# A decode kernel's extra w2 row: four transfers into a rotated buffer in place of three into its own, and one VectorE operation fewer per attention output

## The chip, the cores and the metric

One core of one Trainium2 chip runs the kernel. The metric is the device time of that core in microseconds, the median of several executions. The kernel before takes 135.47 us (three executions: 135.47 to 135.51). The profile of one more execution, of 135.52 us, shows a span of 133.7 us from the first to the last instruction; all positions below are microseconds from the start of that span.

## The reference

A single decode step for two batch rows of width 576: layer norm of `x`, then attention over a cached window and a dense MLP with a squared ReLU, both from the same normed input, and everything is added up.

```python
W = min(4096, max(256, Sk // 4))                 # 2048 of Sk = 8192 cached positions
q = (xn @ wq).reshape(B, 1, 32, 128)             # B = 2, 32 query heads on 16 kv heads
k, v = k_cache[:, :, Sk-W:], v_cache[:, :, Sk-W:]  # each (2, 16, 2048, 128) bf16
p = softmax(q . k * 128 ** -0.5)
a = (p . v).reshape(B, 1, 4096) @ wo             # wo 4096 x 576
h = relu(xn @ w1 + b1); h = h * h                # w1 576 x 4608
m = h @ w2 + b2                                  # w2 4608 x 576
out = x + a + m
```

All inputs and the output are bf16. Keys and values come to 33.6 MB, the four weight matrices to 20 MB, and each byte is read once.

## The kernel before

Attention is cut into eight units `u` of four kv heads and one batch row. Each unit has one key tile and one value tile of 2 MB, in a pool of six. The large transfers are issued on the queue of SyncE (SP), the small ones on ScalarE's (ACT).

```python
XS = [(0, 85), (85, 117), (117, 128)]
W2P = [(0, 9), (9, 14), (14, 16), (16, 17)]       # pieces of the second half of w2
...
kvpool = ctx.enter_context(tc.tile_pool(name="kvpool", bufs=6))
keep = ctx.enter_context(tc.tile_pool(name="keep", bufs=2))
...
const.tile([P, 112], F32, name="pad_0")
w2x_sb = const.tile([P, D], BF16, name="w2x_sb")  # D = 576: 1152 bytes in each of 128 rows
xb_sb = const.tile([B + 1, D], BF16, name="xb_sb")
nc.scalar.dma_start(out=x_sb, in_=x2d)            # two rows
load_k(0); wq_sb = issue_flat(A_wq, "wq"); load_k(1); load_v(0); load_k(2); load_v(1); load_k(3)
...
def softmax(u):
    ...                                           # row maxima, exponentials into p_sb
    pT = keep.tile([P, NJJ, SR], BF16, tag="pT", name=f"pT_{u}")
    nc.vector.transpose(out=pT[:].rearrange("p j r -> p (j r)"), in_=p_sb[:])
...
def fin():                                        # the end of one unit: normalise, spread into ws
    op = psum.tile([P, Dh + 1], F32, tag="op", name=f"op_ps_{u}")
    matmul(op[pp, :], lhsT=of_h[:], rhs=o1[:], ...)
    nc.vector.reciprocal(out=linv[pp, :], in_=op[pp, Dh:Dh + 1])
    mk = work.tile([P, WC], F32, tag="mk", name=f"mk_{u}")
    nc.vector.tensor_scalar(out=mk[pp, :], in0=own_c[pp, :], scalar1=linv[pp, 0:1], ...)
    nc.vector.tensor_tensor(out=om, in0=op[pp, 0:Dh]..., in1=mk[pp, :]...to_broadcast([32, WC, WR]), op=ALU.mult)
    nc.vector.tensor_reduce(out=ws[pp, :, BS * b], in_=om..., op=ALU.add)
```

The main sequence. `step(u)` transposes the keys of unit `u` on TensorE, multiplies the probabilities of unit `u - 2` by its values, and computes scores and softmax of `u`.

```python
softmax(0)
load_v(2)
for i in range(0, 2 * NG4, 4):                    # b1: 8 rows of 1152 bytes, four at a time
    nc.scalar.dma_start(out=b1_sb[i:i + 4, :], in_=b1_rows[i:i + 4, :])
nc.scalar.dma_start(out=xb_sb[B:B + 1, :], ...)   # b2: one row
for p0, p1 in XS:                                 # the extra row of w2
    nc.scalar.dma_start(out=w2x_sb[p0:p1, :], in_=w2_rows[1, p0:p1, (FR - 1) * D:FR * D])
step(1)
...
for u in range(2, NU - 1):
    step(u)
    ...                                           # v, k and, at u == 4, w1 issued as buffers come free
mlp_h(w1_sb)
wo_sb = issue_flat(A_wo, "wo")
...                                               # w2a, w2b and three pieces of w2c issued
step(NU - 1)
pv_all(NU - 2)
out_acc(hT_sb[:, 1, FR - 1, :], w2x_sb, 0)        # the one use of w2x_sb
pv_all(NU - 1)
for r in range(WR):
    out_acc(ws[:, r, :], wo_sb, r)
for r in range(FR):
    out_acc(hT_sb[:, 0, r, :], w2a_sb, r)
for r in range(FR - 1):
    w, o = (w2b_sb, r) if r < r9 else (w2c_sb, r - r9)
    out_acc(hT_sb[:, 1, r, :], w, o, stop=(r == FR - 2))
nc.scalar.copy(out=fin_sb[:], in_=out_ps[:])
nc.scalar.dma_start(out=..., in_=fin_sb[0:RM:BS, :])
```

Of the kernel before, what the change touches and what calls it, by code (L numbers as in the profile page):

```python
# [8 lines left out]
F32 = mybir.dt.float32  # L9
BF16 = mybir.dt.bfloat16  # L10
ACT = mybir.ActivationFunctionType
ALU = mybir.AluOpType
# [4 lines left out]
def kernel(  # L17
# [14 lines left out]
    nc = tc.nc  # L32
    P = 128
    B, Sq, D = A_x.shape
    _, Hkv, Sk, Dh = A_k_cache.shape
# [19 lines left out]
    NJJ = NJ // NS  # L55
    SR = NS * NC
# [4 lines left out]
    NG4 = 4  # L61
# [10 lines left out]
    WR = Hq * Dh // P  # L72
    WC = Dh // WR
    FR = L1 // P
    assert HW == 32 * FR and QH * 2 == NC and NC * WC == 32
    W2P = [(0, 9), (9, 14), (14, 16), (16, 17)]
    XS = [(0, 85), (85, 117), (117, 128)]
    BS = 16
    MB = BS * (B - 1) + 1
    RM = 32 * (NG4 - 1) + MB  # L80
# [3 lines left out]
    const = ctx.enter_context(tc.tile_pool(name="const", bufs=1))  # L84
# [4 lines left out]
    work = ctx.enter_context(tc.tile_pool(name="work", bufs=2))  # L89
    keep = ctx.enter_context(tc.tile_pool(name="keep", bufs=2))  # L90
# [22 lines left out]
    def load_v(u):  # L113
        issue_kv(v_tiles, A_v_cache, u, "v")

    def issue_flat(w, name):
# [2 lines left out]
        nc.sync.dma_start(out=tl[:, 0:n], in_=w.rearrange("r n -> (r n)").rearrange("(p l) -> p l", p=P))  # L119
        return tl  # L120

    const.tile([P, 112], F32, name="pad_0")
    w2x_sb = const.tile([P, D], BF16, name="w2x_sb")
    xb_sb = const.tile([B + 1, D], BF16, name="xb_sb")
    x_sb = xb_sb[0:B, :]
    nc.scalar.dma_start(out=x_sb, in_=x2d)
# [16 lines left out]
                                 op0=ALU.mult, op1=ALU.add)  # L143
# [3 lines left out]
    for q in range(4):  # L147
        nc.vector.tensor_scalar_add(out=row_f[32 * q:32 * (q + 1), :], in0=row32[32 * q:32 * (q + 1), 0:1],
                                    scalar1=float(32 * q))
# [21 lines left out]
    for k in range(NK):  # L171
        nc.vector.tensor_scalar(out=xn_sb[:, k, :].rearrange("b (m c) -> b m c", c=2), in0=x_v[:, :, k:k + NK:NK - 1],  # L172
                                scalar1=mv[:, 0:1], scalar2=rstd[:, 0:1], op0=ALU.subtract, op1=ALU.mult)
# [7 lines left out]
    for t0, half, k0, n, pc in ((0, 0, 0, NK, 0), (0, 1, 0, NK, 1), (1, 0, 1, NK - 1, 1), (1, 1, 0, NK - 1, 0)):  # L181
        nc.vector.tensor_scalar(out=xnT[:, t0:NH:2, half, :], in0=pro_ps[:, k0:k0 + n, :], scalar1=par[:, pc:pc + 1],
                                scalar2=None, op0=ALU.mult)
# [3 lines left out]
    own_c = const.tile([P, WC], F32, name="own_c")  # L187
# [5 lines left out]
                          in_=own[:].unsqueeze(2).to_broadcast([P, NC, WC]))  # L193
    in_s = const.tile([P, NS], F32, name="in_s")
    nc.vector.tensor_reduce(out=in_s[:], in_=ident[:].rearrange("p (g s c) -> p s g c", s=NS, c=NC), axis=AX.XY,
                            op=ALU.add)
    far_h = const.tile([TH, P], BF16, name="far_h")
    nc.vector.tensor_scalar(out=far_h[:].rearrange("p (a h r) -> p a h r", h=TH, r=rep),
                            in0=ident[0:TH, 0:TH].unsqueeze(1).unsqueeze(3).to_broadcast([TH, P // NC, TH, rep]),
# [87 lines left out]
    def softmax(u):  # L287
        sc_ps = sc_tiles.pop(u)
        m1 = work.tile([P, 1], F32, tag="m1", name=f"m1_{u}")
        nc.vector.tensor_reduce(out=m1[:], in_=sc_ps[:], axis=AX.X, op=ALU.max)  # L290
        m2 = work.tile([P, NC], F32, tag="m2", name=f"m2_{u}")
        nc.vector.tensor_scalar(out=m2[:], in0=off[:], scalar1=m1[:, 0:1], scalar2=None, op0=ALU.add)  # L292
        gmax = work.tile([P, NC], F32, tag="gmax", name=f"gmax_{u}")
        nc.gpsimd.partition_all_reduce(gmax[:], m2[:], channels=P, reduce_op=ReduceOp.max)  # L294
        gown = work.tile([P, NC], F32, tag="gown", name=f"gown_{u}")
        bias = work.tile([P, 1], F32, tag="bias", name=f"bias_{u}")
        nc.vector.scalar_tensor_tensor(out=gown[:], in0=gmax[:], scalar=-scale, in1=own[:], op0=ALU.mult,  # L297
                                       op1=ALU.mult, accum_out=bias[:])
        p_sb = work.tile([P, NJJ * 32], BF16, tag="p_sb", bufs=1, name=f"p_{u}")
        o1 = keep.tile([P, Dh + 1], F32, tag="o1", name=f"o1_{u}")  # L300
        nc.scalar.activation(out=p_sb[:], in_=sc_ps[:], func=ACT.Exp, bias=bias[:, 0:1], scale=scale,  # L301
                             accum_out=o1[:, Dh:Dh + 1])
        pT = keep.tile([P, NJJ, SR], BF16, tag="pT", name=f"pT_{u}")
        nc.vector.transpose(out=pT[:].rearrange("p j r -> p (j r)"), in_=p_sb[:])  # L304
        pT_tiles[u] = pT
        o1_tiles[u] = o1
# [18 lines left out]
    def pv_end(u):  # L325
        tq, b = divmod(u, B)
        o_ps = o_tiles.pop(u)
        o1 = o1_tiles.pop(u)
        for k in range(NS):
            kw = dict(out=o1[:, 0:Dh], in0=o_ps[:, k * Dh:(k + 1) * Dh])  # L330
            if k == 0:
                nc.vector.tensor_scalar(scalar1=in_s[:, 0:1], scalar2=None, op0=ALU.mult, **kw)  # L332
            else:
                nc.vector.scalar_tensor_tensor(scalar=in_s[:, k:k + 1], in1=o1[:, 0:Dh], op0=ALU.mult, op1=ALU.add,  # L334
                                               **kw)

        def fin():
            op = psum.tile([P, Dh + 1], F32, tag="op", name=f"op_ps_{u}")
            pp = slice(32 * tq, 32 * (tq + 1))
            matmul(op[pp, :], lhsT=of_h[:], rhs=o1[:], start=True, stop=True, skip_group_check=True,  # L340
                   tile_position=(0, 32 * tq))
            linv = work.tile([P, 1], F32, tag="linv", name=f"linv_{u}")
            nc.vector.reciprocal(out=linv[pp, :], in_=op[pp, Dh:Dh + 1])
            mk = work.tile([P, WC], F32, tag="mk", name=f"mk_{u}")
            nc.vector.tensor_scalar(out=mk[pp, :], in0=own_c[pp, :], scalar1=linv[pp, 0:1], scalar2=None, op0=ALU.mult)
            om_t = work.tile([P, Dh], F32, tag="om", name=f"om_{u}")
            om = om_t[pp, :].rearrange("p (q r) -> p q r", r=WR)
            nc.vector.tensor_tensor(out=om, in0=op[pp, 0:Dh].rearrange("p (q r) -> p q r", r=WR),
                                    in1=mk[pp, :].unsqueeze(2).to_broadcast([32, WC, WR]), op=ALU.mult)
            with nc.allow_low_precision(reason="sums of one term and zeros"):  # L350
                nc.vector.tensor_reduce(out=ws[pp, :, BS * b], in_=om.rearrange("p q r -> p r q"), axis=AX.X,
                                        op=ALU.add)

        return fin

    def mlp_h(w1_sb):
        h_ps = [psum.tile([P, HB], F32, tag="kT", bufs=3, name=f"h_ps_{k}") for k in range(2)]
        for k in range(2):
            matmul(h_ps[k][:], lhsT=sel_h[:], rhs=b1_sb[:, k * HB:(k + 1) * HB], start=True, stop=False,
                   skip_group_check=True)  # L360
        for t in range(NH):
            for k in range(2):
                for g in range(NG4):
                    o = t * L1 + g * HW + k * HB
                    matmul(h_ps[k][32 * g:32 * g + 2 * B, :],
                           lhsT=xnT[:, t].rearrange("p x b -> p (x b)"), rhs=w1_sb[:, o:o + HB], start=False,
                           stop=(t == NH - 1), skip_group_check=True, tile_position=(0, 32 * g))
        hrow = const.tile([RB, 4 * HW], BF16, tag="row", name="hrow")
        h4 = hrow[:].rearrange("p (a n) -> p a n", a=4)
        for k in range(2):  # L370
            t1_t = work.tile([P, HB], F32, tag="t1", name=f"t1_{k}")
            t1 = t1_t[0:RB, :]
            nc.scalar.activation(out=t1, in_=h_ps[k][0:RB, :], func=ACT.Relu)  # L373
            t4 = t1.unsqueeze(1).to_broadcast([RB, 4, HB])
            nc.vector.tensor_tensor(out=h4[:, :, k * HB:(k + 1) * HB], in0=t4, in1=t4, op=ALU.mult)  # L375
        nr = FR // 2
        for a in range(2):
            hp = psum.tile([P, nr, RB + 4], BF16, tag="sc", bufs=2, name=f"hp_{a}")
            for r in range(nr):
                transpose(out=hp[:, r, 0:RB], in_=hrow[:, a * nr + r:4 * HW:FR], identity=ident[0:RB, 0:RB])  # L380
            for g in range(NG4):
                pp = slice(32 * g, 32 * (g + 1))
                cp = nc.scalar.copy if g % 2 else nc.vector.tensor_copy
                cp(out=hT_sb[pp, :, a * nr:(a + 1) * nr, 0:MB:BS].rearrange("p x r b -> p r x b"),
                   in_=hp[pp, :, 32 * g:32 * g + 2 * B].rearrange("p r (x b) -> p r x b", b=B))
# [28 lines left out]
    softmax(0)  # L414
    load_v(2)
    b1_rows = B_b1.rearrange("(x n) -> x n", n=HW)
    for i in range(0, 2 * NG4, 4):
        nc.scalar.dma_start(out=b1_sb[i:i + 4, :], in_=b1_rows[i:i + 4, :])
    nc.scalar.dma_start(out=xb_sb[B:B + 1, :], in_=B_b2.rearrange("(o n) -> o n", o=1))
    for p0, p1 in XS:  # L420
        nc.scalar.dma_start(out=w2x_sb[p0:p1, :], in_=w2_rows[1, p0:p1, (FR - 1) * D:FR * D])
    step(1)
    load_k(4)
    out_acc(sel_b[:], xb_sb, 0, start=True)
    for u in range(2, NU - 1):
        step(u)
        if u + 1 < NU - 2:
            load_v(u + 1)
        if u == 4:
            w1_sb = issue_flat(B_w1, "w1")  # L430
        if u + 3 < NU:
            load_k(u + 3)
        if u == 5:
            for v in (NU - 2, NU - 1):
                load_v(v)
    mlp_h(w1_sb)
    wo_sb = issue_flat(A_wo, "wo")
    w2a_sb = w2pool.tile([P, FR * D], BF16, name="w2a")
# [52 lines left out]
```

## Time and profile before

| what | before |
|---|---|
| time, median of 3 | 135.47 us |
| span of the profile | 133.7 us |
| TensorE matmuls busy | 85.7 us (64%) |
| VectorE busy | 64.6 us (48%) |
| ScalarE busy | 46.7 us (35%) |
| GpSimd busy | 4.9 us (4%) |
| moved by DMA | 53.76 MB, mean 402 GB/s |
| granted TensorE clock, mean | 0.82 |

A row of the page that divides the span into 40 slices gives the busy share of each engine and of the 16 DMA engines in tenths. "The chain that ended last" follows the last instruction back through what released each step. A group line names a source line, engine, operation and tiles, then the count, the busy time, the mean of one in ns, and the idle time before it with what ended it. "SPq" and "ACTq" are the sequencers that issue transfers. Beside the instructions the trace records every DMA packet (queue, start, duration, size) and the moment of each completion mark; a transfer leaves one mark for each DMA engine that took part, and, where fewer than 16 did, one early mark[...].

### The profile page before, as it was taken

The numbers are of one execution on the slowest core, as the hardware profiler recorded it, in microseconds if no ns is written. First come the engines' busy times: TensorE is split into PE (matmuls) and PEld (weight loads), VectorE is DVE, ScalarE is ACT, GpSimd is POOL, SyncE is SP. The second block draws the span as 40 slices with busy tenths as digits, with TensorE's granted clock in tenths as the row PEclk, the third lists the DMA queues.
The fourth block names the chain that finished last, engine by engine and source line by source line (L and its number), as shares of the span: only waits on it lengthen the run. The fifth ranks groups of instructions, "written<-read, shape, count | busy, mean of one in ns | idle before, by whom it ended". The sixth has DMA issues, their size and how long they took to land.

```text
span 133.7 us, 2291 instructions
## 1 busy us (share of the span) xinstructions
PE 85.7 (64%) x949; PEld 53.5 (40%) x949; DVE 64.6 (48%) x184; ACT 46.7 (35%) x67; POOL 4.9 (4%) x15
## 2 busy tenths in 40 slices
PE   0079419599598497599779778204729971739461
PEld 0069302287354263336436444002427530228350
DVE  7754400354567587437657767620065767540000
ACT  5715400339476174244356176010206632000000
POOL 5000000010000100100010000100000001000000
PEclk9999955868999999757999999755686998555955
DMA  4999989999999999999999999999999998999940
GB/s 153 382 449 472 424 360 405 431 412 412 424 436 421 441 421 436 426 436 426 436 426 424 436 477 409 464 419 392 421 441 421 458 490 386 415 428 409 395 163 1
DMA packets 3660, 53.76 MB, mean 402 GB/s; under 512 B 439, under 2 KB 706, under 8 KB 962
## 3 DMA queue, kind: packets, MB, share of 16 engines
q1 hardware_dynamic: 3456, 53.46, 94.3%
q10 hardware_dynamic: 194, 0.16, 0.4%
q8 instruction: 7, 0.11, 0.3%
q14 instruction: 3, 0.02, 0.0%
HBM read 53.62 MB, written 0.00 MB: 401 GB/s over the span
## 4 chain that ended last, share of the span: by engine, by line
DMA 77%; PE 17%; SPq 2%; DVE 1%; ACT 1%; issue 1%; ACTq 0%; DVEq 0%
DMA w2c<-in_B_w_dram 24%; DMA w<-in_B_w_dram 23%; DMA k<-in_A_k_cache_dram 16%; DMA wq<-in_A_wq_dram 14%; PE kT_ps L97 6%; PE h_ps L94 3%; PE q_ps L94 3%; PE o_ps L94 1%; PE sc_ps L94 1%; PE out_ps L94 1%; SPq L106 1%; DVE qrow L237 1%; ACT qrow L237 0%; DVE qz L253 0%; SPq L442 0%
## 5 line engine op out<-in xcount | busy, mean ns | idle before, releaser
L97 PE MATMUL kT_ps<-ident_f,k 128*128 128x128 f32 x256 | 42.3, 318 | 6.0 <-DMA k<-in_A_k_cache_dram 4.0
L97 PEld LDWEIGHTS kT_ps<-ident_f,k 128*128 128x128 f32 x256 | 34.0, 164 | 19.0 <-issue 11.5
L269 ACT COPY kT<-kT_ps 128x1024 bf16<-128x1024 bf16 x32 | 31.9, 1012 | 19.3 <-PE kT_ps L97 19.2
L271 DVE COPY kT<-kT_ps 128x1024 bf16<-128x1024 bf16 x32 | 21.8, 680 | 6.8 <-PE kT_ps L97 6.6
L94 PE MATMUL sc_ps<-kT,qz 128*32 128x512 bf16 x128 | 9.7, 383 | 7.4 <-DVE kT L271 5.5
L301 ACT ACTIVATE p<-sc_ps,bias 128x512 bf16<-128x512 f32 x8 | 5.5, 687 | 22.2 <-DVE gown L297 22.1
L94 PE MATMUL o_ps<-v,pT 128*32 128x512 bf16 x128 | 11.6, 444 | 0.0
L94 PEld LDWEIGHTS <-xnT 128*4 128x4 bf16 x108 | 3.5, 119 | 15.8 <-issue 14.2
L94 PE MATMUL h_ps<-w,xnT 128*4 128x288 bf16 x72 | 4.2, 421 | 7.0 <-DMA w<-in_B_w_dram 7.0
L304 DVE STREAM_TRANSPOSE pT<-p 128x512 bf16<-128x512 bf16 x8 | 5.7, 710 | 6.1 <-ACT p L301 6.1
L334 DVE SCALAR_TENSOR_TENSOR o<-o_ps,in_s,o 128x128 f32<-128x128 f32 x24 | 8.3, 344 | 0.4
L290 DVE TENSOR_REDUCE m<-sc_ps 128x1 f32<-128x512 f32 x8 | 5.5, 692 | 4.6 <-PE sc_ps L94 4.6
L94 PE MATMUL q_ps<-wq,xnT 128*4 128x512 bf16 x36 | 4.0, 627 | 4.9 <-DMA wq<-in_A_wq_dram 4.9
L294 POOL PARTITION_ALL_REDUCE gmax<-m x8 | 2.9, 365 | 106.0 <-DVE m L292 106.0
L375 DVE TENSOR_TENSOR hrow<-t 100x1152 bf16<-100x1152 f32 x2 | 2.6, 1355 | 8.5 <-ACT t L373 8.5
L459 ACT CAST fin_sb<-out_ps 113x144 bf16<-113x144 f32 x1 | 0.3, 279 | 18.3 <-PE out_ps L94 18.3
L94 PE MATMUL op_ps<-o,of_h 128*32 128x129 f32 x16 | 3.7, 316 | 4.6 <-DVE o L334 4.6
L94 PEld LDWEIGHTS <-qz 128*32 128x32 bf16 x128 | 2.1, 94 | 11.1 <-DVE kT L271 8.0
L97 PE MATMUL pro_ps<-ident,xn_sb 2*128 2x2 bf16 x5 | 0.9, 181 | 6.8 <-DVE xn_sb L172 6.5
L94 PEld LDWEIGHTS <-hT_sb 128*17 128x17 bf16 x144 | 3.4, 106 | 4.2 <-issue 4.0
L332 DVE TENSOR_SCALAR o<-o_ps,in_s 128x128 f32<-128x128 f32 x8 | 2.7, 343 | 4.2 <-PE o_ps L94 4.2
L237 DVE CAST qrow<-q_ps 100x512 bf16<-100x512 f32 x1 | 0.7, 691 | 8.2 <-PE q_ps L94 8.2
(73 smaller groups left out, 60.5 us busy)
## 6 DMA issues: line engine op xcount, KB each, us to landing
k<-in_A_k_cache_dram SPq DMA_DIRECT2D x8, 2048.0 KB, 19.4
v<-in_A_v_cache_dram SPq DMA_DIRECT2D x8, 2048.0 KB
w<-in_B_w_dram SPq DMA_DIRECT2D x1, 5184.0 KB, 30.9
wq<-in_A_wq_dram SPq DMA_DIRECT2D x1, 4608.0 KB, 18.2
wo<-in_A_wo_dram SPq DMA_DIRECT2D x1, 4608.0 KB, 21.2
w2a<-in_B_w_dram SPq DMA_DIRECT2D x1, 2592.0 KB
w2b<-in_B_w_dram SPq DMA_DIRECT2D x1, 1296.0 KB
w2c<-in_B_w_dram SPq DMA_DIRECT2D x1, 720.0 KB
```

What stands on the lines that cost most here:

```text
L94: tc.keep_in_program_order(nc.tensor.matmul(*a, **k))
L97: tc.keep_in_program_order(nc.tensor.transpose(*a, **k))
L237: cp(out=qrow[:, k * QW:(k + 1) * QW].rearrange("p (i a d) -> p i a d", a=2, d=Dh), in_=q_ps[0:RB, k * QW // 2:(k + 1) * QW // 2].rearrang ...
L269: nc.scalar.copy(out=kT, in_=kT_ps[:])
L271: nc.vector.tensor_copy(out=kT, in_=kT_ps[:])
L290: nc.vector.tensor_reduce(out=m1[:], in_=sc_ps[:], axis=AX.X, op=ALU.max)
L294: nc.gpsimd.partition_all_reduce(gmax[:], m2[:], channels=P, reduce_op=ReduceOp.max)
L301: nc.scalar.activation(out=p_sb[:], in_=sc_ps[:], func=ACT.Exp, bias=bias[:, 0:1], scale=scale, accum_out=o1[:, Dh:Dh + 1])
L304: nc.vector.transpose(out=pT[:].rearrange("p j r -> p (j r)"), in_=p_sb[:])
L332: nc.vector.tensor_scalar(scalar1=in_s[:, 0:1], scalar2=None, op0=ALU.mult, **kw)
L334: nc.vector.scalar_tensor_tensor(scalar=in_s[:, k:k + 1], in1=o1[:, 0:Dh], op0=ALU.mult, op1=ALU.add, **kw)
L375: nc.vector.tensor_tensor(out=h4[:, :, k * HB:(k + 1) * HB], in0=t4, in1=t4, op=ALU.mult)
```

## The change

The tile of the extra w2 row is no longer a constant of its own. It takes one turn in the buffers of the transposed probabilities `pT`, of which there are three in place of two, and is asked for after `step(6)`, so its transfers wait for a buffer. They are four, of 25, 25, 64 and 14 rows, in place of three of 85, 32 and 11. The bias `b1` comes in one transfer of eight rows in place of two of four, so ScalarE's queue issues as many transfers as before. The padding tile grows by 128 bytes. In `fin`, one operation multiplies by the reciprocal and by the mask; the scaled mask `mk` goes away. No byte more or less is read, and no result is left out.

```diff
-    XS = [(0, 85), (85, 117), (117, 128)]
+    XS = [(0, 25), (25, 50), (50, 114), (114, 128)]
...
-    const.tile([P, 112], F32, name="pad_0")
-    w2x_sb = const.tile([P, D], BF16, name="w2x_sb")
+    const.tile([P, 144], F32, name="pad_0")
...
-        pT = keep.tile([P, NJJ, SR], BF16, tag="pT", name=f"pT_{u}")
+        pT = keep.tile([P, NJJ, SR], BF16, tag="pT", bufs=3, name=f"pT_{u}")
...
-            mk = work.tile([P, WC], F32, tag="mk", name=f"mk_{u}")
-            nc.vector.tensor_scalar(out=mk[pp, :], in0=own_c[pp, :], scalar1=linv[pp, 0:1], scalar2=None, op0=ALU.mult)
...
-            nc.vector.tensor_tensor(out=om, in0=op[pp, 0:Dh].rearrange("p (q r) -> p q r", r=WR),
-                                    in1=mk[pp, :].unsqueeze(2).to_broadcast([32, WC, WR]), op=ALU.mult)
+            nc.vector.scalar_tensor_tensor(out=om, in0=op[pp, 0:Dh].rearrange("p (q r) -> p q r", r=WR),
+                                           scalar=linv[pp, 0:1], op0=ALU.mult, op1=ALU.mult,
+                                           in1=own_c[pp, :].unsqueeze(2).to_broadcast([32, WC, WR]))
...
-    for i in range(0, 2 * NG4, 4):
-        nc.scalar.dma_start(out=b1_sb[i:i + 4, :], in_=b1_rows[i:i + 4, :])
+    for i in range(0, 2 * NG4, 8):
+        nc.scalar.dma_start(out=b1_sb[i:i + 8, :], in_=b1_rows[i:i + 8, :])
...
-    for p0, p1 in XS:
-        nc.scalar.dma_start(out=w2x_sb[p0:p1, :], in_=w2_rows[1, p0:p1, (FR - 1) * D:FR * D])
     step(1)
...
             for v in (NU - 2, NU - 1):
                 load_v(v)
+    w2x_sb = keep.tile([P, D], BF16, tag="pT", bufs=3, name="w2x_sb")
+    for p0, p1 in XS:
+        nc.scalar.dma_start(out=w2x_sb[p0:p1, :], in_=w2_rows[1, p0:p1, (FR - 1) * D:FR * D])
     mlp_h(w1_sb)
```

## The prediction

> **What bounds the kernel now.** I read the chain that ended last first, then its last pieces, the busy time by stretch, the DMA queues, and last the trace's single packets and completion marks. The chain, by engine and by line, and its end (start, length, what):
>
> ```profile
> DMA 77%; PE 17%; SPq 2%; DVE 1%; ACT 1%; issue 1%; ACTq 0%; DVEq 0%
> ...
> 97.64 31.76 DMA w2c<-in_B_w_dram
> 129.40 0.04 issue
> 129.44 1.41 PE out_ps L94 x32
> 130.85 0.02 issue
> 130.88 0.28 ACT fin_sb L459
> ```
>
> Three quarters of the chain are transfers, and the end hangs on the last pieces of w2: 32 short matmuls, a copy and the store follow their landing. Is the DMA idle anywhere before it? By stretch (window, length, PE, PEld, DVE, ACT, POOL busy, clock, DMA share, GB/s):
>
> ```profile
> 30.00:40.00 10.00, 8.14 (x78) 5.34 (x76) 5.54 (x14) 7.46 (x10) 0.36 (x1) 0.95 1.00 424
> 70.00:80.00 10.00, 8.01 (x74) 4.85 (x75) 7.31 (x20) 5.49 (x8) 0.36 (x1) 1.00 1.05 449
> 105.00:115.00 10.00, 6.11 (x69) 3.18 (x71) 7.28 (x22) 2.80 (x4) 0.36 (x1) 0.89 1.01 435
> 115.00:125.00 10.00, 5.83 (x160) 4.32 (x156) 2.95 (x10) 0.00 (x0) 0.00 (x0) 0.59 0.96 408
> 125.00:129.60 4.60, 2.77 (x108) 2.07 (x100) 0.00 (x0) 0.00 (x0) 0.00 (x0) 0.67 0.74 297
> 129.60:134.00 4.40, 1.23 (x32) 0.73 (x24) 0.00 (x0) 0.28 (x1) 0.00 (x0) 0.50 0.01 3
> ```
>
> The share is about 1 to 125 us: no hole that an earlier issue could fill. It falls to 0.74 in the last stretch. There the 16 engines finish one after another, and the slowest sets the end. The completion marks of the last piece of w2c show it, one for each engine:
>
> ```
> 127.66 127.67 127.82 127.94 128.00 | 128.35 128.44 128.61 128.98 129.20 | 129.36 129.38 129.49 129.51 129.52 | 130.49
> ```
>
> One engine lands 0.97 us after all others. **The end of this kernel is the queue of one DMA engine.** All large transfers have 128 rows and give each engine the same bytes, so only the small ones differ. The queues (packets, MB, share of 16 engines):
>
> ```profile
> q1 hardware_dynamic: 3456, 53.46, 94.3%
> q10 hardware_dynamic: 194, 0.16, 0.4%
> q8 instruction: 7, 0.11, 0.3%
> q14 instruction: 3, 0.02, 0.0%
> ```
>
> q10 is ScalarE's queue (x, b1, b2, w2x); q8 and q14 are fetches of instructions. They are tiny as a mean, but not spread evenly.
>
> [...]the 85-row transfer leaves 5 marks, the 32-row one 16, the 11-row one 11, each 4-row one of b1 4, and b2's row 1. Which engines they are it doesn't say, but in the value load that landed from 29.33 to 30.51 us, 11 marks lie within 0.42 us and 5 come 0.29 to 0.76 us after them: five engines carry the 85 rows. [...]about 20 us w2x packets follow each other on an engine by 0.68 us, which is one 16 KB packet (0.611) and one of 1152 bytes (0.051). [...]the trace has seven such packets on q8, 875 to 1072 ns long, about 258 TensorE instructions apart.
>
> **Who the last engine is.** Pieces of w2x per engine before: engines 0 to 4 take 17 + 2 + 1 = 20 packets, 5 to 10 take 2 + 1 = 3, 11 to 15 take 2. Engine 0 also has one row of x, two of b1 and one of b2: 24 packets. I strung the packets into 16 sequences by size and end-to-start times; the one that ends last (130.04, then the mark at 130.49) holds 24 packets of 1152 bytes, and the q14 fetches at 35.90 and 123.26. The marks support it: between the landings of wo and w2a one engine, already among the latest, falls back by 1.06 us more. So I take the last engine to be engine 0. The stringing is an inference; sequences that stand even can be exchanged.
>
> **The change part by part.**
>
> *Split of the row.* After: 25 rows go to 5 engines, 5 each; the next 25 likewise; 64 to 16, 4 each; 14 to 14, 1 each. Engines 0 to 4 take 5 + 5 + 4 + 1 = 15, 5 to 13 take 5, 14 and 15 take 4 (75 + 45 + 8 = 128). Engine 0: 5 packets fewer, 5 x 0.051 = 0.26 us off the path. The others gain at most 3 packets, 0.15 us, and end 0.97 us earlier than engine 0: nothing.
>
> *b1 in one transfer.* Eight rows on eight engines: engine 0 has one packet fewer, 0.05 us. Completion packets (9 ns) number seven on engine 0 before and after.
>
> *Later transfer.* Waiting for a pT buffer moves w2x from 9 to 31 us to about 79 us on: the eighth allocation of three buffers takes that of unit 4, and unit 4's products end in step 6, at 78.4 us by the timeline. During w1 a turn takes 41472 / 16384 x 0.611 + 0.051 = 1.6 us, later 0.66. Engine 0 needs 15 packets and 4 completions: 8 turns by w1's landing at 92, 11 x 0.66 = 7 us more, about 99 to 100. Its use by TensorE is at 113.67: hidden, with 13 us to spare. For an engine that never idles, the order of its packets doesn't matter: 0.
>
> *Semaphores.* SyncE's queue has waits on the small transfers:
>
> ```profile
> SPq L106 <- DMA w2x_sb<-in_B_w_dram: 9.7, 2, 8.6
> SPq L106 <- DMA b_sb<-in_B_b_dram: 4.2, 2, 2.3
> ```
>
> Loads that don't read w2x wait for it, because a completion semaphore is used again after eight transfers (the load at 28.79 was issued 0.08 us after w2x landed). These waits go early, but the DMA was full behind them: 0. In exchange late pieces of w2 may wait for w2x or v. They are needed in the queue only by about 116 us, when wo (landing 117.47) runs out: 0.
>
> *ScalarE.* Four issues at 0.27 to 0.39 us, 1.1 to 1.6 us, fall between its copies in step 6. TensorE stands idle later for w1 (7.0 us in the waits), so up to several us of delay are swallowed: 0.
>
> *VectorE.* Before and after, per output:
>
> ```profile
> L345 DVE TENSOR_SCALAR mk<-own_c,linv x8: 217/220/228, 42.8 to 118.7; 32x4 f32<-32x4 f32 x8
> L348 DVE TENSOR_TENSOR om<-op_ps,mk x8: 278/286/298, 43.0 to 118.9; 32x128 f32<-32x128 f32 x8
> ```
>
> 220 ns go; the three-operand form on 128 elements takes 344 ns at L334, against 286 for the product. Saving 220 - 58 = 162 ns or somewhat more with the gap, 1.3 us of 64.6 over eight. The last one ends at 119.6 us, and what follows it waits for w2a anyway (TensorE, idle in brackets):
>
> ```profile
> 124.69 0.99 PE L94 MATMUL out_ps<-w2a,hT_sb 128*17 128x144 bf16 x51 [1.20 <-DMA w2a<-in_B_w_dram]
> ```
>
> Off the path: 0.
>
> *Sum.* 6 packets x 0.051 = 0.31 us earlier at the last mark, and the tail follows it one to one: 135.47 - 0.31 = 135.16; I say 135.2.
>
> **The rivals.** (a) *The last engine isn't one of engines 0 to 4*, but one that got several q8 fetches. Then it gains 0.1 to 0.15 us of packets: 135.6. Against it: the 24 packets of its sequence; for it: those fetches cost about 1.45 us each by the marks, more than all of w2x. (b) *The fetch at 123.26 moves.* It costs engine 0 about 1 us close to the end, and I don't know what asks for it. If it falls elsewhere, or after the last piece, the next marks at 129.52 become the end: up to 1 us less, 134.5. If another comes behind the transfers, as the q8 fetch at 127.50 now does on an engine already done, it could cost as much: 136. (c) *The rotated buffer or the semaphores become a wait that empties the DMA queue*: w2x is late, TensorE stalls in step 6 or at 113.67. Against it are the 13 us above and 7 us of TensorE's idle time; it would need an issue placed on ScalarE so early that it holds up the copies of a whole step. Then 137 to 140. (d) *VectorE's saving counts*: only if scores bound the loads; with the DMA share at 1 it doesn't.
>
> **Range and chances.** The sum moves by a third of a microsecond, the fetches by one either way: 134.4 to 135.8 eight times in ten. 2% are 2.7 us, more than anything above but (c): faster 0.02, same 0.95, slower 0.03.
>
> **What would show it.** Right: w2x issued near 79 us and landed by 102; the DMA share still near 1 from 2 to 125 us; the last mark about 0.3 us earlier and nearer to the second last (0.6 to 0.7 us); VectorE busy about 1.3 us less with no effect on the end; the wait for w2x gone from SyncE's early loads. Wrong: a drop of the DMA share before 125, a wait of TensorE for w2x, an end moved by a fetch instead of packets, or another engine at the end.

## The result and the profile after

The kernel after takes 134.71 us (median of four executions, 134.68 to 134.83), the kernel before, timed beside it, 135.47 us. The ratio is 0.9946, 95% interval 0.9929 to 0.9963: 0.76 us, or 0.54%, faster. The span of the profile went from 133.7 to 132.8 us. Times below are medians that leave out executions over 1.5% slower than their kernel's fastest, each ratio is to the kernel before on the same chip, and one profile alone, that of the kernel with `mk` put back, is of such a slow execution (137.49 us).

The chain that ended last, by engine, and its last pieces (start, length, what), of the kernel after:

```profile
DMA 62%; PE 21%; ACT 7%; DVE 5%; issue 2%; POOL 1%; SPq 0%; ACTq 0%; POOLq 0%; DVEq 0%
...
100.00 28.51 DMA w2c<-in_B_w_dram
128.51 0.04 issue
128.55 1.41 PE out_ps L94 x30
129.95 0.02 issue
129.98 0.28 ACT fin_sb L458
```

The tail is the same, and all of it is 0.90 us earlier (129.98 for the last copy, against 130.88). The lower DMA share says only that the chain now runs back through a semaphore of w2x at 100.00 us and through its issue at 85; the DMA was no less busy than before. The busy time by stretch (columns as in the prediction) shows that:

```profile
30.00:40.00 10.00, 7.91 (x74) 4.95 (x72) 5.39 (x13) 6.88 (x11) 0.36 (x1) 0.95 1.01 427
70.00:80.00 10.00, 8.35 (x79) 4.42 (x78) 7.28 (x20) 5.63 (x7) 0.36 (x1) 1.00 1.07 460
105.00:115.00 10.00, 6.29 (x70) 3.29 (x68) 7.03 (x20) 2.80 (x4) 0.36 (x1) 0.89 0.98 421
115.00:125.00 10.00, 6.15 (x185) 4.80 (x180) 2.31 (x7) 0.00 (x0) 0.00 (x0) 0.59 0.97 413
125.00:129.60 4.60, 2.86 (x86) 2.19 (x87) 0.00 (x0) 0.00 (x0) 0.00 (x0) 0.67 0.72 287
129.60:134.00 4.40, 0.33 (x8) 0.10 (x3) 0.00 (x0) 0.28 (x1) 0.00 (x0) 0.50 0.00 1
```

The DMA share (last but one) stays near 1 up to 125 us, as before. What differs is how the 16 engines finish. The completion marks of the last w2c piece, one for each DMA engine, in us:

```
before 127.66 127.67 127.82 127.94 128.00 128.35 128.44 128.61 128.98 129.20 129.36 129.38 129.49 129.51 129.52 130.49
after  127.76 127.86 127.94 127.96 128.17 128.20 128.31 128.32 128.86 129.08 129.32 129.39 129.43 129.47 129.57 129.59
```

Place by place the first fifteen moved by at most 0.3 us either way. The one at 130.49 is gone. And one row of the DMA queues has changed (packets, MB, share):

```profile
q8 instruction: 7, 0.11, 0.3%
q14 instruction: 2, 0.02, 0.0%
```

Before, q14 had three fetches, at 35.90, 72.24 and 123.25 us. Now there are two, at 36.66 and 73.70. The third, after which one engine fell 1.06 us back, doesn't happen. The waits of SyncE's queue changed as the edit intends: the early loads no longer wait for w2x, the late pieces of w2 do.

```profile
SPq L485 <- DMA w2b<-in_B_w_dram: 24.6, 1, 24.6
SPq L106 <- PE kT_ps L97: 23.5, 6, 10.4
...
SPq L444 <- DMA w2x_sb<-in_B_w_dram: 3.8, 2, 2.8
```

VectorE is busy 63.1 us in place of 64.6. The merged operation, as the trace gives it by line:

```profile
L345 DVE SCALAR_TENSOR_TENSOR om<-op_ps,linv,own_c x8: 339/346/360, 43.7 to 118.1; 32x128 f32<-32x128 f32 x8
```

Three theories for the 0.76 us: **F**, the third q14 fetch belongs to VectorE and goes away with eight of its instructions, of which the page counts 176 in place of 184; **P**, engine 0 has six packets fewer, as predicted; **R**, the early loads, no longer held by semaphores of small transfers, bring it.

### The profile page after: what moved, and what is told of

Its sections match the earlier page's. It is cut to its first block, busy times and chain, and to the rows that moved or that the text cites. A ratio compares the mean times of both kernels' runs of the same rounds, so it can differ in the third digit from the quotient of the medians.

```text
span 132.8 us, 2285 instructions
## 1 busy us (share of the span) xinstructions
PE 86.4 (65%) x949; PEld 52.6 (40%) x949; DVE 63.1 (47%) x176; ACT 46.6 (35%) x67; POOL 4.9 (4%) x15
## 4 chain that ended last, share of the span: by engine, by line
DMA 62%; PE 21%; ACT 7%; DVE 5%; issue 2%; POOL 1%; SPq 0%; ACTq 0%; POOLq 0%; DVEq 0%
DMA w2c<-in_B_w_dram 21%; DMA k<-in_A_k_cache_dram 16%; DMA wq<-in_A_wq_dram 13%; DMA w2x_sb<-in_B_w_dram 11%; PE kT_ps L97 10%; PE sc_ps L94 5%; ACT kT L268 4%; PE q_ps L94 3%; ACT p L300 2%; DVE m L289 2%; PE out_ps L94 1%; DVE kT L270 1%; ACT L300 1%; PE qT_ps L97 1%; POOL gmax L293 1%
## 5 line engine op out<-in xcount | busy, mean ns | idle before, releaser
L97 PE MATMUL kT_ps<-ident_f,k 128*128 128x128 f32 x256 | 41.0, 310 | 5.3 <-ACT kT L268 2.7
L97 PEld LDWEIGHTS kT_ps<-ident_f,k 128*128 128x128 f32 x256 | 32.4, 159 | 19.2 <-issue 8.7
L94 PE MATMUL sc_ps<-kT,qz 128*32 128x512 bf16 x128 | 10.5, 414 | 6.5 <-DVE kT L270 4.7
L94 PE MATMUL out_ps<-wo,ws 128*17 128x144 bf16 x128 | 4.0, 325 | 1.1 <-DVE ws L349 1.1
```

The costliest lines, as they stand in the source:

```text
L94: tc.keep_in_program_order(nc.tensor.matmul(*a, **k))
L97: tc.keep_in_program_order(nc.tensor.transpose(*a, **k))
```

## The experiments

### The parts apart

First the kernel before with only the merged operation.

```diff
# kernel before
-            mk = work.tile([P, WC], F32, tag="mk", name=f"mk_{u}")
-            nc.vector.tensor_scalar(out=mk[pp, :], in0=own_c[pp, :], ...)
-            nc.vector.tensor_tensor(out=om, ...)
+            nc.vector.scalar_tensor_tensor(out=om, ...)
```

> The kernel before, with only the merged VectorE operation (8 VectorE instructions fewer); w2x, b1 and the two pT buffers as before. Theory F (the third q14 fetch, at 123.26 us before and absent after, is VectorE's own and goes away with 8 instructions): no q14 packet after 100 us, no straggler in the marks of the last w2c piece, the last mark at about 129.5 in place of 130.49, time 134.5 to 134.8. Theory P (packets of w2x on engine 0, as predicted): the third fetch and the straggler stay, 135.4 to 135.5. Theory R (the early loads, no longer held up by semaphores of small transfers, give the gain): 135.4 to 135.5.

Measured: 134.70 us, ratio 0.9940 (0.9927 to 0.9953), the whole gain of the change. Its queues:

```profile
q10 hardware_dynamic: 194, 0.16, 0.4%
q8 instruction: 7, 0.11, 0.3%
q14 instruction: 2, 0.02, 0.0%
```

Two fetches on q14, no late mark (the last is 129.64, the one before it 129.54). The small transfers are those of before (194 packets on q10), and SyncE's queue still waits for w2x:

```profile
SPq L106 <- DMA w2x_sb<-in_B_w_dram: 9.6, 2, 8.6
```

So neither P nor R is needed for the gain. Next, the kernel before with only the new split and the single transfer of b1.

```diff
# kernel before
-    XS = [(0, 85), (85, 117), (117, 128)]
+    XS = [(0, 25), (25, 50), (50, 114), (114, 128)]
-    for i in range(0, 2 * NG4, 4):
-        nc.scalar.dma_start(out=b1_sb[i:i + 4, :], in_=b1_rows[i:i + 4, :])
+    for i in range(0, 2 * NG4, 8):
+        nc.scalar.dma_start(out=b1_sb[i:i + 8, :], in_=b1_rows[i:i + 8, :])
```

> The kernel before, with only the new split of w2x (25, 25, 64, 14 rows) and b1 in one transfer; still issued early, in its own tile, mk kept. Theory P: 6 packets of 0.051 us fewer on engine 0, straggler stays and lands 0.31 us earlier: about 135.16. Theory F with P: the same, 135.1 to 135.2. Theory F alone: 135.4 to 135.5. Theory R: early loads still share semaphores with small transfers, so 135.4 to 135.5.

Measured: ratio 0.9985 (0.9972 to 0.9998), 0.2 us faster, with an interval from 0.03 to 0.38 us. The third fetch is there, at 123.37 us:

```profile
q10 hardware_dynamic: 202, 0.16, 0.4%
q8 instruction: 7, 0.11, 0.3%
q14 instruction: 3, 0.02, 0.0%
```

The last mark lies 0.71 us behind the one before it, against 0.97 before: 0.26 us nearer, where 0.31 was predicted. That fits the packet count, but doesn't show it: the last mark itself is at 130.60, no earlier than before, in an execution of 135.74 us where the median is 135.43, and the gain in time could be 0.03 us as well as 0.38. Then the kernel after with `mk` put back, everything else kept.

```diff
# kernel after
+            mk = work.tile([P, WC], F32, tag="mk", name=f"mk_{u}")
+            nc.vector.tensor_scalar(out=mk[pp, :], in0=own_c[pp, :], ...)
-            nc.vector.scalar_tensor_tensor(out=om, ...)
+            nc.vector.tensor_tensor(out=om, ...)
```

> The kernel after, with the separate mk operation put back (8 VectorE instructions more), everything else as after. Theory F with P: the third q14 fetch is back near 122 to 123 us and falls on one engine, a straggler of 0.5 to 0.7 us in the last marks, time 135.1 to 135.2. Theory R, or the packets alone: no straggler, 134.7 as after.

Measured: ratio 0.9984 (0.9974 to 0.9994), with the third fetch at 123.48 us. Late transfers, new split and third pT buffer together give no more than the split gave alone. Last, the kernel after with the old split and b1 in two transfers.

```diff
# kernel after
-    XS = [(0, 25), (25, 50), (50, 114), (114, 128)]
+    XS = [(0, 85), (85, 117), (117, 128)]
-    for i in range(0, 2 * NG4, 8):
-        nc.scalar.dma_start(out=b1_sb[i:i + 8, :], in_=b1_rows[i:i + 8, :])
+    for i in range(0, 2 * NG4, 4):
+        nc.scalar.dma_start(out=b1_sb[i:i + 4, :], in_=b1_rows[i:i + 4, :])
```

> The kernel after, with the old split of w2x (85, 32, 11 rows) and b1 in two transfers; late, in a pT buffer, mk merged. Theory F: without the third fetch engines 0 to 4 are not the last, and the six engines that got a q8 fetch have 2 to 3 packets fewer: last mark 129.4 to 129.6, time 134.6 to 134.75. Theory P: six packets more on engine 0, 0.31 us slower than after: 135.0. Theory R: 134.7.

Measured: 134.84 us, ratio 0.9947 (0.9934 to 0.9960), the same as the kernel after. Without the third fetch the new split is worth nothing that these runs resolve. Whatever w2x does, the two kernels of these four without `mk` take 134.7 to 134.84 us, and the two with it have ratios of 0.9985 and 0.9984.

### The operation, or the number of instructions?

Idle memsets on VectorE give the kernel after its old number of instructions back and leave the merged operation as it is; four in place of eight go half way.

```diff
# kernel after
     nc.vector.memset(eps_t[:], 1e-5)
+    idle = const.tile([B, 1], F32, name="idle")
+    for _ in range(8):                        # 4 in the second kernel
+        nc.vector.memset(idle[:], 0.0)
```

> The kernel after, with eight memsets of one element on VectorE at the very start that nothing reads, so VectorE has as many instructions as before while the merged operation stays. If the number of VectorE instructions decides on the third q14 fetch: a q14 packet near 122 to 124 us again, a straggler of 0.5 to 0.7 us in the last marks, time 135.2 to 135.5, as with mk back. If the merged operation itself, or a shorter end of each attention output, gives the gain: no third fetch, 134.7 to 134.9.

> The kernel after, with four such idle memsets, half way between the two lengths of VectorE's program. If a count decides: one of two states and nothing between, either the third fetch and 135.2 to 135.5, or none and 134.7 to 134.9. If each VectorE instruction costs something on its own: about 135.05, half of the difference.

Measured on one chip: eight memsets 136.14 us (ratio 1.0047, 1.0035 to 1.0059), four 135.55 us (1.0000, 0.9992 to 1.0009). With eight, the third fetch is back at 122.98 us, and the last mark (131.14) is 0.84 us behind the one before it. With four there is a third fetch too, but at 134.88 us, after the kernel's last instruction; the last seven marks lie within 0.43 us. The two kernels differ in nothing but four memsets of about 0.06 us at the very start, and the step between them is 0.59 us. The ends of the marks, four memsets and eight:

```
four   ... 129.90 130.12 130.26 130.34 130.36 130.49 130.52 130.55
eight  ... 129.82 130.11 130.18 130.21 130.22 130.27 130.30 131.14
```

The times alone wouldn't rule out that each instruction costs something: the first four memsets cost 0.8 us beside the kernel after, the next four 0.59. The packets do. Those of SyncE's queue, summed and divided by 16 engines, take 126.0 us in the kernel after, 126.8 with four memsets and 126.6 with eight. So the first 0.8 us is longer packets on every engine, and the second step is not: there one mark alone is late. The queues with four, then with eight:

```profile
q1 hardware_dynamic: 3456, 53.46, 94.8%
q14 instruction: 2, 0.02, 0.0%
```

```profile
q1 hardware_dynamic: 3456, 53.46, 94.2%
q14 instruction: 3, 0.02, 0.0%
```

So VectorE's count of instructions decides. In all 14 traces of this case the third fetch goes by it: none with 176 busy VectorE instructions on the page (eight traces), after the end with 180 (one), at 122.7 to 123.5 us with 184 (five). That the fetch is VectorE's own is argued from this, as the packets don't say for whom they are.

Both kernels are slower than expected by some 0.7 us more, on all engines alike. The edit wasn't clean: the `idle` tile moved every later tile, and the key and value tiles went from address 31232 of each partition to 31264, 32 bytes further. From 31 to 60 us, with four memsets, 165 of 751 packets of 16 KB then took more than 620 ns, against 3 of 761 in the kernel after. The address as the cause was not tried by itself. The next run puts the kernel after beside the eight memsets.

```diff
# the kernel after, unchanged
```

> The kernel after, unchanged, beside the next three on one chip: 134.7 to 134.9, two q14 fetches, marks of the last piece within 1.9 us. The kernels with idle memsets and with two transfers all had packets that took up to 0.8% longer (16 KB: 623 to 625 ns, against 620). If this kernel has that too here, it belongs to the chip or the run and not to those edits: then 135.3 to 135.6.

Measured: 134.75 us, ratio 0.9950 (0.9930 to 0.9969), 16 KB packets of 620 ns on the mean. For the kernels with memsets (623 to 625) the slower packets are those of the edit, not of the chip.

> The kernel after with eight idle memsets on VectorE, beside the kernel after: if the number of VectorE instructions decides on the third fetch, slower than it by 0.5 to 0.8 us, with a q14 packet near 123 us and one late mark. If not: the same time.

Measured beside it: 136.19 us, ratio 1.0043 (1.0029 to 1.0057), the fetch at 122.73 us. Its last mark is 0.38 us behind the one before it, less than the 0.84 of the other execution. Of the 1.44 us, 0.6 is the fetch by the step above; about 0.8 came with the moved tiles, as four memsets show (135.55).

### What the split does

If other engines than 0 to 4 are last now, loading engines 0 to 4 more should help. This edit was meant to do that.

```diff
# kernel after
-    XS = [(0, 25), (25, 50), (50, 114), (114, 128)]
+    XS = [(0, 100), (100, 128)]
```

> The kernel after, with w2x in two transfers of 100 and 28 rows: 22 packets on each of engines 0 to 4, 2 on engines 5 to 13, none on 14 and 15. If the last six marks belong to engines past 4 that a q8 fetch has put back: they lose 3 packets, 0.15 us, and engines 0 to 4 gain 7, 0.36 us, up to about 129.4: last mark about 129.45, time 134.55 to 134.65, 0.1 to 0.15 us better than after. If engines 0 to 4 are among the last six: 0.3 us slower, 135.0.

> The kernel after with w2x in transfers of 100 and 28 rows, beside the kernel after: if the last six marks are those of engines past 4 put back by q8 fetches, 0.1 to 0.15 us faster than it; if engines 0 to 4 are among them, 0.3 us slower.

Measured: ratios 0.9987 (0.9969 to 1.0005) and 0.9986 (0.9965 to 1.0008), 135.05 and 134.97 us, spread over 134.66 to 136.34. No gain; slower than the kernel after by 0.2 to 0.3 us, but with such a spread that no size can be given. The 16 KB packets took 625 ns on the mean in one profiled execution (135.58 us) and 619 in the other (134.66), so the spread goes with them. Both expectations had the edit wrong, however. Beside the early mark, the 100-row transfer left 10 marks and not 5: ten engines carried 10 rows each, so none had 22 packets. With the numbering that the prediction uses, which is an estimate from counts of marks, engines 0 to 4 have 12 packets in place of 15 and engines 5 to 9 have 12 in place of 5. These runs say nothing on a heavier load of engines 0 to 4.

Next, one transfer of all 128 rows; its 16 marks mean 8 packets on each engine:

```diff
# kernel after
-    XS = [(0, 25), (25, 50), (50, 114), (114, 128)]
+    XS = [(0, 128)]
```

> The kernel after with w2x in one transfer of 128 rows, 8 packets on each engine. If the last six engines are past 4: they gain 3 to 4 packets, 0.15 to 0.2 us slower than the kernel after. If engines 0 to 4 are the last: they lose 7 packets, 0.35 us faster.

Measured: **134.42 us**, ratio 0.9918 (0.9904 to 0.9931), 0.33 us faster than the kernel after beside it: the best of all. This is the sign that was written down for "engines 0 to 4 are the last", but not for that reason. Its 16 marks, from 127.19 to 129.06, lie at 128.04 on the mean, against 128.75 for the kernel after beside it, and place by place every one is earlier by 0.45 to 1.13 us. So the gain is not that of five engines alone. Windows from 92.5 to 106 us, in which most of w2x moves beside the last value loads, first of the kernel after as it ran beside the others, then with one transfer:

```profile
92.50:106.00 13.50, 10.56 (x119) 6.75 (x111) 6.08 (x12) 4.46 (x9) 0.00 (x0) 0.72 1.05 436
```

```profile
92.50:106.00 13.50, 10.47 (x123) 6.76 (x114) 6.64 (x13) 4.99 (x9) 0.00 (x0) 0.77 1.05 448
```

The rate (last column) rises from 436 to 448 GB/s. By single packets: with one transfer all 307 packets of 16 KB in that window took 611 ns, with the split of the kernel after 632.6 on the mean, over 620 ns in 168 of 312. The number of packets for each engine, or which engine writes which rows? Two halves of 64 rows keep the number.

```diff
# kernel after
-    XS = [(0, 25), (25, 50), (50, 114), (114, 128)]
+    XS = [(0, 64), (64, 128)]
```

> The kernel after with w2x in two transfers of 64 rows: 4 + 4 = 8 packets on each engine, as with one of 128 rows[...]. With one transfer of 128 rows all 16 KB packets from 92.5 to 106 us took 611 ns and the time was 134.42 us; with the splits of before and after they took 632 to 645 on the mean. If the number of packets for each engine is what counts (many on a few engines keep two queues alternating for long): 611 ns again and 134.4 to 134.5. If it is which engine writes which partitions: 630 to 650 ns and 134.7 to 134.9.

Measured: 134.84 us, ratio 0.9951 (0.9939 to 0.9964); 624.5 ns on the mean, 63 of 308 packets lengthened. That mean lies between the two expectations because the window begins too late: two halves lengthen packets from 90 us on. From 86 to 110 us, with 384 packets of 16 KB in each trace, the mean is 631 ns with two halves, 633 with the kernel after and 611 with one transfer. Each half left 16 marks, so every engine again had 4 + 4 = 8 packets, and the longer packets are back and the gain of the single transfer is gone: the number for each engine isn't the cause. Which rows an engine writes is what remains of the two, and was not shown: no trace tells which engine wrote which rows, and that there are two transfers in place of one was not held apart from it. The runs show the longer packets, not their cause.

## Why the prediction was right, and where not

The time fell in the range, but not by the sum. Of the prediction's own signs of being wrong one came true, "an end moved by a fetch instead of packets": the end moved by 0.90 us, not 0.3, and the last mark is 0.02 us behind the second last, not 0.6 to 0.7.

**The bound** held: DMA share near 1 to 125 us, and the end set by one engine's queue. In the kernel after the DMA is still the limit, but no engine is alone: the last six marks lie within 0.28 us (129.31 to 129.59).

**"Off the path: 0" for VectorE is the step that failed.** Its time is off the path: the merged operation takes 346 ns in place of 220 + 286, 160 ns less for each output, and TensorE still waits for w2a:

```profile
123.71 0.98 PE L94 MATMUL out_ps<-w2a,hT_sb 128*17 128x144 bf16 x50 [0.78 <-DMA w2a<-in_B_w_dram]
```

But eight instructions fewer kept a fetch out of the kernel, and that was worth 0.6 us between the two memset kernels and all 0.8 us in the kernel with the merged operation alone, where only the last mark moved (130.49 to 129.64; the mean of all 16 went from 128.78 to 128.83). The prediction had the fetch, its engine's delay of 1.06 us and the height of the next marks (129.52; the last is now 129.59), and put it all in rival (b) as a thing that might move by chance. That the number of instructions had changed on one engine was known, and was not set beside the fetch.

**6 packets x 0.051 = 0.31 us.** Not refuted while the late engine was late: 0.26 us by the distance of the marks, 0.2 us (0.03 to 0.38) by the times of the split alone. In the kernel after it counts for nothing, as the engine that it relieves isn't the last by a microsecond any more; the gains don't add.

**"The order of its packets doesn't matter: 0"** is right in the sum, by two errors of one size. A misplaced w2x packet costs more than its 51 ns: beside w2x, 16 KB packets took 640.1 ns from 20 to 31 us before, and 638.0 from 92.5 to 106 us after, against 611. That is 0.49 and 0.52 us for each engine. The cost was moved, not removed; the kernel before with merged operation and early transfers is as fast as the change (134.70 us).

**Semaphores, ScalarE, the rotated buffer: 0.** Right. In the trace before, all 438 marks lie on eight semaphores, and the value load issued at 28.79 us leaves its marks (48.74 to 50.67) on the one where w2x's 85 rows landed at 28.71. The transfers were issued from 84.8 to 86.1 us, not 79, as they came with step 6's exponential on ScalarE (84.73), and landed by 101.3, 12 us before use (113.3). The wait moved to w2c's issue at 100.00, with wo in the queue until 117.

**Rival (a)** isn't settled: the sequence of 24 packets made the late engine likely engine 0, and the split brought it nearer to the others, but no record names it. The numbers of engines are the author's estimate. What the trace after shows is that the four transfers left 5, 5, 16 and 14 marks: those of the first two from 92.08 to 93.06 us and from 95.53 to 96.44, and of each of the others five late ones, 98.94 to 99.98 (the other 11 by 93.36) and 100.36 to 101.31 (the other nine by 94.67). So it seems that the same five engines take part in all four, whichever they are. **Rivals (c) and (d)** are out. The distance of the q8 fetches, about 258 TensorE instructions, is a mean: the six gaps are 144 to 364 instructions of the trace, weight loads included.

**The range.** 134.71 lies in 134.4 to 135.8. The centre missed by 0.45 us: it had 0.31 us of packets, which count for nothing in the kernel after, and left out the fetch. The range was wide enough because rival (b) was in it, with the right size (the marks at 129.52 become the end) and no cause. That the fetch fell behind the end and not before it was, for the prediction, luck.

## What to carry to other kernels

Here the DMA share stayed near 1 to 125 us, and the end was that of the slowest single engine (its mark at 130.49 us before, the next at 129.52). In such a kernel read the completion marks of the last transfer one by one, and look for what fell on the last engine alone, fetches of instructions included. Instructions taken off an engine with time to spare paid here by their number (eight on VectorE, ratio 0.9940). A small tile can move the large ones, here from 31232 to 31264, and packets were longer after that move (165 of 751 over 620 ns, against 3 of 761), so an edit that adds instructions needs a control that keeps the addresses. Count the marks of a split before reasoning from it: 100 rows went over ten engines, not five. A small transfer beside large ones went best here with their own shape, all 128 rows (134.42 us).

## What the runs showed of the hardware that was not expected

A third fetch of 8 KB on q14, 309 to 325 ns as a packet, left one mark 0.38 to 0.97 us behind all others in four traces, and came before the end with 184 VectorE instructions on the page and not with 176 or 180. In the windows read here, small transfers of other than 128 rows lengthened the 16 KB packets of other transfers from 611 to means of 624 to 669 ns, both ends from the split in 100 and 28 rows, and one of 128 rows didn't at all (611). In the kernel with four memsets, whose key and value tiles began at 31264 in place of 31232, a fifth of the 16 KB packets from 31 to 60 us took over 620 ns (165 of 751).
